# The gradient of the gate's taps: from full 128-channel blocks to 32-channel blocks at four column positions

## The chip, the cores and the metric

The kernel runs on one core of one Trainium2 chip. The metric is the device time of one launch in microseconds. The core has a matrix engine (PE, with its weight loads shown apart as PEld), a vector engine (DVE), a scalar engine (ACT), GpSimd (POOL), and a queue engine (SP) that issues most of the DMAs.

## The reference

The reference is the forward pass of a branchformer block and its gradients. B = 2 sequences of T = 4000 tokens have D = 144 channels, and the convolutions have K = 5 taps:

```
xa  = layernorm(x)
q, k, v = xa @ w_qkv                      # full attention over 4000 tokens
glob = softmax(q k^T / sqrt(D)) v @ w_att_out
u, g = gelu(xa @ w_mlp_in)                # two halves of 144 channels
g   = layernorm(g)
gc  = sum_i shift(g, i) * dw_csgu[i]      # 5 taps per channel: the gate
loc = (u * gc) @ w_mlp_out
m   = concat(glob, loc);  m = m + depthwise_conv(m, dw_merge)
out = x + m @ w_merge
```

It returns the output and the gradients of x and of all weights. The one that matters here is the gradient of `dw_csgu`, 5 x 144 numbers: for tap i and channel c it is the sum over all tokens t of g[t + i - 2, c] times the gradient of gc[t, c].

## The kernel before

A sequence is 32 blocks of 125 tokens, block j holding tokens p*32 + j for p = 0 to 124. The attention phase (`phase_att`) goes through 64 row tiles of 125 tokens, one per step s, 32 for each sequence. In a step the kernel computes the scores of tile s and the gradient of the probabilities of tile s - 1 (`quad`, L1186 and L1193: eight matmuls, of which four use all 128 rows and four use 16 rows each at four row positions), the softmax (L1208 on DVE, L1214 on ACT), the product with the gradient (L1224 on ACT, L1225 on DVE), two transposes by DMA (`PT`, `ST`), the products with them (`yz`, L1235 and L1274), and the accumulation of the gradient of the normalised input (`X_group`, L1330, added by DVE at L1337).

Beside attention runs the local branch (`local_units`): for sequence 0 in steps 2 to 26, for sequence 1 in steps 34 to 60. It works on groups of two blocks, and it is a list of small units that the steps take in equal shares. `ring` holds, for each block, the normalised gate g (`ring[:, 0]`) and the gradient of gc (`ring[:, 1]`), so that a block's five shifted copies are five neighbouring slots.

After every second group the tap gradient is taken for four blocks. The kernel multiplies `ring[:, 1]` of a block, as weights, with the five shifted blocks of `ring[:, 0]`, all 128 x 128 channel pairs, of which only the diagonal is wanted in the end. `dwc_unit(g, 0)` does four matmuls of 128 x 512 (four taps; L707). `dwc_unit(g, 1)` does, for each of the four blocks, one of 128 columns (the fifth tap; L709) and one for the last 16 channels, with channels 32 to 143 as weights and 80 columns (L710). Each sums in a PSUM buffer of the pool `ps_w`, which has three buffers and is shared with X, the projections and the gate. `flush` then copies the PSUM tile to `fl` on ACT (L693) and adds it on POOL to `A.dwc` (L694), a 128 x 720 accumulator in SBUF. `dwi_unit` does the same for the gradient of `w_mlp_in` (L722), with the same `fl`. A unit of the tap gradient runs 8 times per sequence, 16 times in all.

At the very end `Final.dwc` takes the diagonals: five DVE operations of 128 x 128 with the identity (L1831), five of 16 x 16 (L1833), two casts, two transposes on PE, one copy, one DMA.

The order of the instructions on each engine is written out: `Planner.ORDER` has one list per engine. The program is first emitted in program order and cut into runs. A run is one instruction, or on PE up to 16 consecutive matmuls into one tensor, or up to eight score matmuls. `plan` then chains the runs in the order of the list.

Of the kernel before, what the change touches and what calls it, by code (L numbers as in the profile page):

```python
# [8 lines left out]
BF = mybir.dt.bfloat16  # L9
F32 = mybir.dt.float32  # L10
ACT = mybir.ActivationFunctionType
ALU = mybir.AluOpType
# [3 lines left out]
D = 144  # L16
DR = 16
# [498 lines left out]
G2 = 2  # L516
# [5 lines left out]
def local_units(k, W, b, S, A, es, DHT, ps_w, gw):  # L522

    nc, tc = k.nc, k.tc
# [5 lines left out]
    ring = pl.tile([PB, 2, 16, D], BF, name="ring")  # L530
# [25 lines left out]
    fl = pl.tile([128, 512], F32, name="l_fl")  # L556
# [134 lines left out]
    def flush(ps, r0, r1, acc):  # L691
        n = ps.shape[1]
        nc.scalar.copy(fl[r0:r1, 0:n], ps)  # L693
        nc.gpsimd.tensor_tensor(acc, fl[r0:r1, 0:n], acc, op=ALU.add)  # L694

    def blocks(g):
        return [(g - 1, 0), (g - 1, 1), (g, 0), (g, 1)]

    def dwc_unit(g, part):
        pw = ps_w.tile([128, 512], F32, tag="w")  # L700
        bl = blocks(g)
        for n_, (gg, bi) in enumerate(bl):
            first, last = n_ == 0, n_ == len(bl) - 1
            t = ring[:, 1, (G2 * gg + bi + 2) % 12, :]
            p = (G2 * gg) % 12 + bi
            if part == 0:
                nc.tensor.matmul(pw[:].rearrange("p (a b) -> p a b", b=128), t[:, 0:128], ring[:, 0, p:p + 4, 0:128], start=first, stop=last)  # L707
            else:
                nc.tensor.matmul(pw[:, 0:128], t[:, 0:128], ring[:, 0, p + 4, 0:128], start=first, stop=last, skip_group_check=True)  # L709
                nc.tensor.matmul(pw[0:112, 128:208], t[:, 32:D], ring[:, 0, p:p + 5, 128:D], start=False, stop=last, skip_group_check=True)  # L710
        if part == 0:
            flush(pw[:], 0, 128, A.dwc[:, 0:512])
        else:
            flush(pw[:, 0:128], 0, 128, A.dwc[:, 512:640])
            flush(pw[96:112, 128:208], 96, 112, A.dwc[96:112, 640:720])

    def dwi_unit(g):
        pw = ps_w.tile([96, 3 * D], F32, tag="w")
        bl = blocks(g)
        for n_, (gg, bi) in enumerate(bl):  # L720
            for ct in range(3):
                nc.tensor.matmul(pw[:, ct * D:(ct + 1) * D], dhr[gg % 2][0:PB, bi, ct * 96:(ct + 1) * 96], S.xa_aug[:, G2 * gg + bi, 0:D],  # L722
                                 start=(n_ == 0 and ct == 0), stop=(n_ == len(bl) - 1), skip_group_check=True)
        flush(pw[:], 0, 96, A.dWiT[:])
# [6 lines left out]
    def round_(n, o):  # L731
# [4 lines left out]
        if o is not None and o % 2:  # L736
            end += [(dwc_unit, o, 0), (dwc_unit, o, 1), (dwi_unit, o)]
# [38 lines left out]
class Planner:  # L776

    ORDER = {
# [1156 lines left out]
def kernel(ctx, tc, x, w_qkv, w_att_out, w_mlp_in, dw_csgu, w_mlp_out, dw_merge, w_merge, grad_out,  # L1935
# [47 lines left out]
    A = K()  # L1983
# [194 lines left out]
```

## Time and profile before

| | before |
|---|---|
| median of 3 runs | 1206.63 us (1204.02 to 1208.19) |
| profiled execution | 1207.09 us, span of its instructions 1205.3 us |
| granted TensorE clock | 0.996 |
| PE, DVE, ACT, POOL busy | 1153.0, 1025.6, 934.5, 256.4 us |

Lines such as L707 are lines of the kernel. A row of a group gives line, engine, operation, output and input with shapes, the count, then the busy time in us and the mean of one in ns, then the idle time of that engine just before the group and what ended it. A row of the chain of waits gives the start in us, the length in us and what ran; pieces of the chain lie one behind another, so their lengths are times on the path that ended last. The ends of matmuls are modelled in the profile, so for PE the distance between starts, which the chain shows, says more than the duration of one.

### The profile page before, as it was taken

Reading aid. Unit: us, or ns where it says so; the run is one execution under the profiler, and the core shown is the slowest. Engines: PE = TensorE matmul, PEld = TensorE weight load, DVE = VectorE, ACT = ScalarE, POOL = GpSimd, SP = SyncE. Lnnn points to the kernel's source line nnn. Section 1 sums busy time; section 2 is a strip of 40 time slices with the busy share of each in tenths; the row PEclk is TensorE's granted clock in tenths of the full one; section 3 lists DMA queues with packets and bytes.
Section 4 is the critical chain, followed back from the end, with each engine's and each line's share of the span. In section 5 each row is a group of like instructions: output and inputs, shape, how many; then the busy total and the mean of one; then the engine's idle time right before and its main releaser. Section 6 shows DMA issues by size and latency. Waiting matters only on the chain.

```text
span 1205.3 us, 36108 instructions
## 1 busy us (share of the span) xinstructions
PE 1153.0 (96%) x14352; PEld 896.1 (74%) x14352; DVE 1025.6 (85%) x3035; ACT 934.5 (78%) x1705; POOL 256.4 (21%) x409
## 2 busy tenths in 40 slices
PE   6999999999999989999999999999999899999998
PEld 4667777777777767777777777777777677799997
DVE  8589899999999978778889999999999987667745
ACT  6999888898898765778998789788888657535372
POOL 7111112211212223200111121211112111023450
PEclk9999999999999999999999999999999999999999
DMA  4769888878778898878989888897888979868653
GB/s 116 167 151 181 168 166 170 155 177 163 170 169 160 156 193 175 165 155 187 211 166 171 156 161 168 159 165 156 172 160 150 173 155 179 191 153 212 147 143 89
DMA packets 672570, 198.31 MB, mean 165 GB/s; under 512 B 648339, under 2 KB 666313, under 8 KB 672379
## 3 DMA queue, kind: packets, MB, share of 16 engines
q1 hardware_dynamic: 671270, 194.60, 80.0%
q8 instruction: 112, 1.84, 0.7%
q0 software_dynamic: 592, 1.18, 0.5%
q14 instruction: 58, 0.48, 0.1%
q10 hardware_dynamic: 538, 0.21, 0.1%
HBM read 24.32 MB, written 17.85 MB: 35 GB/s over the span
## 4 chain that ended last, share of the span: by engine, by line
PE 63%; DMA 12%; ACT 11%; DVE 8%; issue 3%; SPq 2%; POOL 1%; DVEq 0%; ACTq 0%; POOLq 0%
PE X L1330 17%; PE ps L1186 12%; PE yz L1274 7%; DMA PT<-Pbuf 7%; PE yz L1235 7%; PE ps L1193 5%; ACT Pbuf L1214 3%; PE Hps L1617 3%; DVE Pbuf L1208 2%; ACT Sbuf L1224 2%; PE po L1715 2%; DMA qt<-qb 1%; DVE Sbuf L1225 1%; PE pd L606 1%; PE pj L1152 1%
## 5 line engine op out<-in xcount | busy, mean ns | idle before, releaser
L1208 DVE TENSOR_SCALAR_CACHE_REDUCE Pbuf<-ps 125x1000 bf16<-125x1000 f32 x256 | 306.5, 1198 | 49.9 <-PE ps L1193 45.1
L1224 ACT CAST Sbuf<-ps 125x1000 bf16<-125x1000 f32 x252 | 253.3, 1005 | 85.4 <-PE ps L1193 67.5
L1214 ACT ACTIVATE Pbuf<-Pbuf,nm 125x1000 bf16<-125x1000 bf16 x256 | 286.6, 1152 | 5.7 <-DVE nm L1210 5.5
L1330 PE MATMUL X<-QBs,Sbuf 125*128 125x144 bf16 x2048 | 280.6, 227 | 0.8 <-ACT l_sq L575 0.3
L1330 PE MATMUL X<-QBs,Pbuf 125*128 125x144 bf16 x2048 | 280.1, 226 | 0.7 <-POOL QBs L1257 0.7
L1186 PE MATMUL ps<-xaT_m,qt 128*128 128x500 bf16 x1024 | 262.4, 376 | 10.8 <-DVE Pbuf L1208 6.2
L1330 PEld LDWEIGHTS <-Sbuf 125*128 125x128 bf16 x2048 | 199.3, 98 | 16.0 <-issue 15.7
L1330 PEld LDWEIGHTS <-Pbuf 125*128 125x128 bf16 x2048 | 200.8, 98 | 2.3 <-issue 1.5
L1225 DVE TENSOR_TENSOR Sbuf<-Sbuf,Pbuf 125x1024 bf16<-125x1024 bf16 x252 | 172.7, 692 | 5.4 <-ACT Sbuf L1224 3.9
L1235 PE MATMUL yz<-xa_aug,PT 125*128 125x145 bf16 x2048 | 151.4, 228 | 16.4 <-DMA PT<-Pbuf 15.5
L1235 PEld LDWEIGHTS <-PT 125*128 125x128 bf16 x2048 | 130.9, 98 | 34.5 <-DMA PT<-Pbuf 22.4
L1274 PE MATMUL yz<-xa_aug,ST 125*128 125x144 bf16 x2048 | 151.1, 228 | 3.8 <-DMA ST<-Sbuf 2.7
L1186 PEld LDWEIGHTS <-qt 128*128 128x128 bf16 x1024 | 92.2, 98 | 77.0 <-issue 12.7
L1274 PEld LDWEIGHTS <-ST 125*128 125x128 bf16 x2048 | 133.0, 98 | 15.6 <-issue 9.0
L1257 POOL TENSOR_TENSOR QBs<-g,g 125x144 bf16<-125x144 f32 x64 | 37.8, 590 | 461.8 <-ACT g L1256 312.4
L1337 DVE TENSOR_TENSOR acc<-X,acc 125x432 f32<-125x432 f32 (+1 forms) x204 | 110.5, 548 | 22.3 <-PE X L1330 22.0
L1193 PEld LDWEIGHTS <-qt 16*128 16x128 bf16 x1024 | 26.3, 91 | 109.7 <-issue 109.7
L1193 PE MATMUL ps<-XR,qt 16*128 16x500 bf16 x1016 | 100.9, 381 | 0.0
L677 POOL TENSOR_SCALAR l_w<-ring,nc,c 125x144 f32<-125x144 bf16 x64 | 34.1, 539 | 165.8 <-DVE nc L673 93.6
L649 DVE TENSOR_TENSOR l_prod<-ring,Wc 125x720 bf16<-125x720 bf16 x128 | 66.1, 538 | 1.9 <-DMA ring<-held 1.6
L1742 ACT ACTIVATE t<-t,dx_c,rstd_x 125x144 f32<-125x144 f32 x64 | 29.2, 501 | 36.5 <-DVE t L1741 29.1
L1617 PE MATMUL Hps<-Yg,go_h 125*128 125x144 bf16 x640 | 54.3, 226 | 0.0
(540 smaller groups left out, 2031.8 us busy)
## 6 DMA issues: line engine op xcount, KB each, us to landing
Yn_d<-yn SPq DMA_DIRECT2D x64, 35.2 KB
Zn_d<-zn SPq DMA_DIRECT2D x64, 35.2 KB
ug_d<-ugr SPq DMA_DIRECT2D x32, 70.3 KB
PT<-Pbuf SPq DMA_TRANSPOSE x126
ST<-Sbuf SPq DMA_TRANSPOSE x126
acc_d<-acc SPq DMA_DIRECT2D x4, 504.0 KB
go_h<-in_grad_out_dram SPq DMA_DIRECT2D x8, 252.0 KB
Yg<-Yn_d SPq DMA_DIRECT2D x8, 252.0 KB
```

Of the source, the lines that this page charges most:

```text
L649: nc.vector.tensor_tensor(prod[:, bi].rearrange("p a b -> p (a b)"), ring[:, a, p + bi:p + bi + 5, :].rearrange("p a b -> p (a b)"), W.Wc[ ...
L1186: mm = nc.tensor.matmul(pp[r // 2][:, r % 2, 0:CH], QT[i][:, 2 * h, :], bs(i)[0].xaT_m[:, c * CH:(c + 1) * CH], start=True, stop=False)
L1193: nc.tensor.matmul(pp[r // 2][:, r % 2, 0:CH], QT[i][rs, 2 * h + 1, :], xr, start=False, stop=True)
L1208: nc.vector.tensor_scalar(pv(pc(i, c2)), src, -1.0, 3.0e38, op0=ALU.mult, op1=ALU.min, accum_out=NM[i][:, c2:c2 + 1])
L1214: nc.scalar.activation(v, v, ACT.Exp, bias=NM[i][:, 4:5], scale=-1.0)
L1224: nc.scalar.copy(pv(sc(i, c2)), src)
L1225: nc.vector.tensor_tensor(sc(i, c2), sc(i, c2), pc(i, c2), op=ALU.mult)
L1235: nc.tensor.matmul(Yw, PT[0:PB, pos(i, j), :], S.xa_aug[:, j, 0:D + 1], start=(j == 0), stop=(j == NB - 1))
L1274: nc.tensor.matmul(Zw, ST[0:PB, j, :], S.xa_aug[:, j, 0:D], start=(j == 0), stop=(j == NB - 1))
L1330: nc.tensor.matmul(X[:, jj, :], l, r, start=(n_ == 0), stop=(n_ == len(ops) - 1))
L1337: nc.vector.tensor_tensor(av, X[0:PB, 0:nj, :], av, op=ALU.add)
L1617: nc.tensor.matmul(H[0:rows, a // 3, (a % 3) * D:(a % 3 + 1) * D], lhs, self.src[b][h][:, 2 + j, :], start=(n == 0 and a % 3 == 0), stop=( ...
```

## The change

The 128 channels are cut into four blocks of 32. The weights of a matmul are 32 channels of `ring[:, 1]`, and its columns are the same 32 channels of the five shifted blocks of `ring[:, 0]`, 160 columns. The result of block c goes to PSUM partitions 32c to 32c + 31, and with that the matmul uses 32 of the array's columns, at one of four positions. Four blocks of tokens times four positions are 16 matmuls. The last 16 channels are done by four more matmuls, one for each block of tokens, each at a position of its own (channels 112 to 143 as weights, 80 columns), so that the four partial sums stay apart. The accumulator is 128 x 240, with one flush per unit. `Final.dwc` takes the diagonals of 32 x 32 blocks, and adds the four partial sums of the last 16 channels with two small matmuls, in two bfloat16 parts.

```diff
-    def dwc_unit(g, part):
-        pw = ps_w.tile([128, 512], F32, tag="w")
-        ...
-            if part == 0:
-                nc.tensor.matmul(pw[:].rearrange("p (a b) -> p a b", b=128), t[:, 0:128], ring[:, 0, p:p + 4, 0:128], start=first, stop=last)
-            else:
-                nc.tensor.matmul(pw[:, 0:128], t[:, 0:128], ring[:, 0, p + 4, 0:128], start=first, stop=last, skip_group_check=True)
-                nc.tensor.matmul(pw[0:112, 128:208], t[:, 32:D], ring[:, 0, p:p + 5, 128:D], start=False, stop=last, skip_group_check=True)
-        if part == 0:
-            flush(pw[:], 0, 128, A.dwc[:, 0:512])
-        else:
-            flush(pw[:, 0:128], 0, 128, A.dwc[:, 512:640])
-            flush(pw[96:112, 128:208], 96, 112, A.dwc[96:112, 640:720])
+    def dwc_unit(g):
+        pw = ps_w.tile([128, 240], F32, tag="w")
+        for q, (gg, bi) in enumerate(blocks(g)):
+            t = ring[:, 1, (G2 * gg + bi + 2) % 12, :]
+            p = (G2 * gg) % 12 + bi
+            for c in range(4):
+                nc.tensor.matmul(pw[32 * c:32 * c + 32, 0:160], t[:, 32 * c:32 * c + 32], ring[:, 0, p:p + 5, 32 * c:32 * c + 32], start=(q == 0), stop=(q == 3), skip_group_check=True)
+        for q, (gg, bi) in enumerate(blocks(g)):
+            ...
+            nc.tensor.matmul(pw[32 * q:32 * q + 32, 160:240], t[:, 112:D], ring[:, 0, p:p + 5, 128:D], start=False, stop=True, skip_group_check=True)
+        flush(pw[:], A.dwc[:])
...
-            end += [(dwc_unit, o, 0), (dwc_unit, o, 1), (dwi_unit, o)]
+            end += [(dwc_unit, o), (dwi_unit, o)]
...
+        for c in range(4):
+            nc.gpsimd.tensor_copy(dg[32 * c:32 * c + 32, :], W.ident[32 * c:32 * c + 32, 32 * c:32 * c + 32])
         for kk in range(5):
-            nc.vector.scalar_tensor_tensor(jf[:, 0:128], av[:, kk * 128:(kk + 1) * 128], 1.0, W.ident[:], ...)
-            nc.vector.scalar_tensor_tensor(jf[96:112, 0:DR], av[96:112, a0:a0 + DR], 1.0, W.ident[96:112, 96:112], ...)
+            nc.vector.scalar_tensor_tensor(jf[:, 0:32], av[:, kk * 32:(kk + 1) * 32], 1.0, dg[:], ...)
+            nc.vector.scalar_tensor_tensor(jf[:, 0:DR], av[:, a0:a0 + DR], 1.0, dg[:, DR:2 * DR], ...)
...
+        nc.tensor.matmul(pr[:], hi[:], dg[:, DR:2 * DR], start=True, stop=False)
+        nc.tensor.matmul(pr[:], lo[:], dg[:, DR:2 * DR], start=False, stop=True)
```

The five lists of `Planner.ORDER` are new throughout. Their lengths go from 1402, 2493, 1711, 405 and 937 runs (PE, DVE, ACT, POOL, SP) to 1402, 2495, 1680, 377 and 937. The local branch has one unit fewer for every second group, so the steps take its units at slightly other places of the program order.

More of the change, by code (lines that the diff above doesn't have):

```diff
@@ L555, in local_units @@
     w_ = pl.tile([PB, G2, D], F32, name="l_w")
-    fl = pl.tile([128, 512], F32, name="l_fl")
+    fl = pl.tile([128, 3 * D], F32, name="l_fl")
     def slot(g):
@@ L689, in dhT_unit, with flush @@
             DHT[G2 * g + bi] = [dhT[:, 3 * bi + ct, :] for ct in range(3)]
[L691 to L694, printed above, removed]
+    def flush(ps, acc):
+        r, n = ps.shape
+        nc.scalar.copy(fl[0:r, 0:n], ps)
+        nc.gpsimd.tensor_tensor(acc, fl[0:r, 0:n], acc, op=ALU.add)
     def blocks(g):
         return [(g - 1, 0), (g - 1, 1), (g, 0), (g, 1)]
-    def dwc_unit(g, part):
-        pw = ps_w.tile([128, 512], F32, tag="w")
-        bl = blocks(g)
-        for n_, (gg, bi) in enumerate(bl):
-            first, last = n_ == 0, n_ == len(bl) - 1
+    def dwc_unit(g):
+        pw = ps_w.tile([128, 240], F32, tag="w")
+        for q, (gg, bi) in enumerate(blocks(g)):
             t = ring[:, 1, (G2 * gg + bi + 2) % 12, :]
             p = (G2 * gg) % 12 + bi
-            if part == 0:
-                nc.tensor.matmul(pw[:].rearrange("p (a b) -> p a b", b=128), t[:, 0:128], ring[:, 0, p:p + 4, 0:128], start=first, stop=last)
-            else:
-                nc.tensor.matmul(pw[:, 0:128], t[:, 0:128], ring[:, 0, p + 4, 0:128], start=first, stop=last, skip_group_check=True)
-                nc.tensor.matmul(pw[0:112, 128:208], t[:, 32:D], ring[:, 0, p:p + 5, 128:D], start=False, stop=last, skip_group_check=True)
-        if part == 0:
-            flush(pw[:], 0, 128, A.dwc[:, 0:512])
-        else:
-            flush(pw[:, 0:128], 0, 128, A.dwc[:, 512:640])
-            flush(pw[96:112, 128:208], 96, 112, A.dwc[96:112, 640:720])
+            for c in range(4):
[5 more added lines that the diff above has]
+        flush(pw[:], A.dwc[:])
     def dwi_unit(g):
@@ L723, in dwi_unit @@
                                  start=(n_ == 0 and ct == 0), stop=(n_ == len(bl) - 1), skip_group_check=True)
-        flush(pw[:], 0, 96, A.dWiT[:])
+        flush(pw[:], A.dWiT[:])
     units = []
@@ L778 @@
     ORDER = {
[54 rows of a table removed]
-        "DVE": [2, 0, 3, 1, 4, 6, 7, 9, 8, 5, 11, 10, 12, 14, 15, 18, 16, 13, 17, 19, 22, 20, 25, 23, 24, 38, 44, 21, 32, 39, 36, 26, 28, 34, 33, 35,
[101 rows of a table removed]
-        "Activation": [1, 4, 0, 9, 10, 7, 8, 15, 34, 12, 11, 14, 13, 16, 39, 5, 42, 18, 19, 20, 3, 22, 21, 2, 23, 29, 28, 6, 24, 25, 17, 32, 26, 31,
[67 rows of a table removed]
-        "Pool": [4, 3, 2, 0, 5, 10, 8, 11, 6, 14, 7, 1, 15, 47, 16, 19, 18, 50, 41, 17, 26, 25, 24, 31, 32, 20, 33, 37, 38, 12, 34, 9, 27, 21, 13,
[48 rows of a table removed]
[54 rows of a table added]
+        "DVE": [2, 3, 0, 1, 4, 11, 5, 9, 10, 8, 7, 6, 12, 14, 15, 21, 16, 13, 17, 20, 22, 42, 24, 18, 44, 19, 25, 23, 32, 60, 34, 26, 28, 36, 33, 35,
[101 rows of a table added]
+        "Activation": [2, 4, 0, 1, 9, 10, 7, 8, 14, 13, 11, 5, 12, 18, 15, 16, 19, 17, 34, 20, 22, 21, 3, 41, 36, 23, 35, 6, 28, 24, 25, 26, 40, 29,
[65 rows of a table added]
+        "Pool": [5, 4, 47, 0, 1, 8, 6, 15, 14, 11, 49, 2, 10, 9, 16, 7, 18, 19, 17, 3, 26, 25, 24, 41, 33, 31, 32, 38, 13, 37, 42, 20, 28, 21, 23,
[47 rows of a table added]
     }
@@ L1828, in dwc @@
         self.jf = jf = fp.tile([128, D], F32, name="jf")
-        av = A.dwc
+        av, dg = A.dwc, fp.tile([128, 32], BF, name="dwc_d")
+        for c in range(4):
+            nc.gpsimd.tensor_copy(dg[32 * c:32 * c + 32, :], W.ident[32 * c:32 * c + 32, 32 * c:32 * c + 32])
         for kk in range(5):
-            nc.vector.scalar_tensor_tensor(jf[:, 0:128], av[:, kk * 128:(kk + 1) * 128], 1.0, W.ident[:], op0=ALU.mult, op1=ALU.mult, accum_out=dwc_c[:, kk:kk + 1])
-            a0 = 640 + kk * DR
-            nc.vector.scalar_tensor_tensor(jf[96:112, 0:DR], av[96:112, a0:a0 + DR], 1.0, W.ident[96:112, 96:112], op0=ALU.mult, op1=ALU.mult, accum_out=dwc_s[96:112, kk:kk + 1])
+            nc.vector.scalar_tensor_tensor(jf[:, 0:32], av[:, kk * 32:(kk + 1) * 32], 1.0, dg[:], op0=ALU.mult, op1=ALU.mult, accum_out=dwc_c[:, kk:kk + 1])
+            a0 = 160 + kk * DR
+            nc.vector.scalar_tensor_tensor(jf[:, 0:DR], av[:, a0:a0 + DR], 1.0, dg[:, DR:2 * DR], op0=ALU.mult, op1=ALU.mult, accum_out=dwc_s[:, kk:kk + 1])
         dwc_b = fp.tile([128, 5], BF, name="dwc_b")
         nc.vector.tensor_copy(dwc_b[:], dwc_c[:])
-        dwc_sb = fp.tile([128, 5], BF, name="dwc_sb")
-        nc.vector.tensor_copy(dwc_sb[96:112], dwc_s[96:112])
-        pt = self.pt([5, D], BF)
-        nc.tensor.transpose(pt[:, 0:128], dwc_b[:], W.ident[:])
-        nc.tensor.transpose(pt[:, 128:D], dwc_sb[96:112], W.ident[96:112, 96:112])
+        hi, lo, lof = fp.tile([128, 5], BF, name="dwc_hi"), fp.tile([128, 5], BF, name="dwc_lo"), fp.tile([128, 5], F32, name="dwc_lf")
+        nc.vector.tensor_copy(hi[:], dwc_s[:])
+        nc.vector.tensor_tensor(lof[:], dwc_s[:], hi[:], op=ALU.subtract)
+        nc.vector.tensor_copy(lo[:], lof[:])
+        pt = self.pt([5, 128], BF)
+        nc.tensor.transpose(pt[:], dwc_b[:], W.ident[:])
+        pr = self.pt([5, DR], F32)
+        nc.tensor.matmul(pr[:], hi[:], dg[:, DR:2 * DR], start=True, stop=False)
+        nc.tensor.matmul(pr[:], lo[:], dg[:, DR:2 * DR], start=False, stop=True)
         o5 = fp.tile([5, D], BF, name="o5")
-        nc.scalar.copy(o5[:], pt[:])
+        nc.scalar.copy(o5[:, 0:128], pt[:])
+        nc.scalar.copy(o5[:, 128:D], pr[:])
         nc.sync.dma_start(k.out5[:, :], o5[:])
@@ L1985 @@
     A.dWiT = ap.tile([96, 3 * D], F32, name="A_dWiT")
-    A.dwc = ap.tile([128, 720], F32, name="A_dwc")
+    A.dwc = ap.tile([128, 240], F32, name="A_dwc")
     k.ps_w = pool(ctx, "ps_w", "left", bufs=3, space=PSUM)
```

535 rows, old and new, of the table ORDER are left out of this document.

## The prediction

> **What bounds the kernel now.** I read the page first, then its chain of waits, then the same two stretches as a table of busy time.
>
> ```profile
> span 1205.3 us, 36108 instructions
> PE 1153.0 (96%) x14352; PEld 896.1 (74%) x14352; DVE 1025.6 (85%) x3035; ACT 934.5 (78%) x1705; POOL 256.4 (21%) x409
> PE 63%; DMA 12%; ACT 11%; DVE 8%; issue 3%; SPq 2%; POOL 1%; DVEq 0%; ACTq 0%; POOLq 0%
> 150.00:400.00 250.00, 247.80 (x3033) 188.38 (x3031) 241.56 (x709) 221.11 (x397) 50.62 (x73) 1.00 0.81 167
> 700.00:900.00 200.00, 196.38 (x2395) 149.09 (x2395) 188.14 (x542) 172.74 (x314) 38.66 (x58) 1.00 0.83 162
> ```
>
> The third line is the share of the chain by engine: TensorE matmuls carry 63% of what ends last. The last two are the middles of the two stages in which the local gate runs beside attention (columns: PE, PEld, DVE, ACT, POOL busy us). There PE has 2.2 and 3.6 us without work. DVE has 8.4 and 11.9 us: it is the next limit, some 4.5% away (20.3 of 450 us). The step that changes, the tap gradient, lies in these stages. One unit of it in the chain (start, us, what):
>
> ```profile
> 229.35 0.86 PE pw L707 x4
> 230.21 0.85 PE ps L1186 x4
> 231.06 0.32 PE ps L1193 x4
> 231.38 1.12 PE yz L1235 x16
> 232.50 0.06 PE pw L709
> 232.56 0.04 PE pw L710
> ...
> 232.87 0.85 PE ps L1186 x4
> ```
>
> The chain runs through PE without a gap here, so PE time removed here is removed from the end, until another engine is late. L707 is the first half of the unit, four matmuls of 512 columns, 0.86 us; L709 and L710 are the second, eight matmuls from 232.50 to 232.87, 0.37 us. Together 1.23 us, and 16 units make 19.7 us. Not all lie on the chain: it passes through L707 in 10 of the 16 units and through L709/L710 in 11; first and last of each:
>
> ```profile
> 134.31 0.86 PE pw L707 x4
> 137.47 0.06 PE pw L709
> ...
> 992.88 0.86 PE pw L707 x4
> 994.12 0.06 PE pw L709
> ```
>
> So I count 0.65 of what PE saves as lying on the path.
>
> **The matmuls.** The unit streams the same columns as before: 4×(512+128+80) = 2880 before, 16×160 + 4×80 = 2880 after. It gains only if the four column positions work at once. No row of this trace has column positions. The nearest has row positions: in the same chain L1186 and L1193 are four matmuls of 500 columns each, 0.85 us one after another on the whole array, and 0.32 us for L1193, whose four use four separate groups of 16 rows. They do overlap. By columns, a full-array matmul costs 0.85/4/500 = 0.425 ns a column, so 160 columns cost 68 ns and 80 columns 34 ns. If four run at once a unit is 4×68 + 34 = 0.31 us, or 4.9 us for 16 units. If all run one after another it is 16×68 + 4×34 = 1.22 us, or 19.6 us: nothing gained. I take the first, because L1193 is the row with the same kind of instruction (part of the array, different positions, back to back). The Trainium skill (TensorE: Matmul & The Clock Gate, Measured speedup vs the span model) gives 2.38 times for three column positions; at that efficiency of 0.79 a unit would be 0.39 us, 6.2 us in all, an estimate that hardly moves the sum.
>
> **Entering and leaving the positions.** L1193 also shows what a change of positions costs. Here a matmul group follows it directly:
>
> ```profile
> 182.35 0.32 PE ps L1193 x4
> 182.68 0.97 PE pw L707 x4
> 183.65 1.01 PE yz L1274 x16
> 184.66 0.85 PE ps L1186 x4
> 185.51 0.32 PE ps L1193 x4
> 185.83 1.12 PE yz L1235 x16
> ```
>
> L707 takes 0.97 behind row positions and 0.86 elsewhere; sixteen yz matmuls take 1.12 and 1.01. So one change costs 0.11 us, and the one into row positions is in L1193's own 0.32 (500 columns alone are 0.21). The new PE list decides how many are added. Numbering its runs in the order in which the program emits them, I find that the 20 matmuls of a unit are two runs, of 16 and of 4. They are neighbours in 9 units and apart in 7; in 15 of 16 the run of 16 stands right behind a group of score matmuls that ends in row positions, and so do the separated runs of 4. There the change is paid already, so each visit adds one, and the odd unit one more: 9 + 2×7 + 1 = 24 changes, 2.6 us. The after-cost is 4.9 + 2.6 = 7.5 us, so PE saves 12.2 us; one after another it would lose 19.6 + 2.6 − 19.7 = 2.5 us. On the path at 0.65 that is 7.9 saved, or 1.6 lost.
>
> **The weight loads.** Twelve loads a unit become twenty of 32 channels.
>
> ```profile
> L1193 PEld LDWEIGHTS <-qt 16*128 16x128 bf16 x1024 | 26.3, 91 | 109.7 <-issue 109.7
> L710 PEld LDWEIGHTS <-ring 125*112 125x112 bf16 x64 | 6.6, 132 | 0.0
> L1235 PE MATMUL yz<-xa_aug,PT 125*128 125x145 bf16 x2048 | 151.4, 228 | 16.4 <-DMA PT<-Pbuf 15.5
> L1235 PEld LDWEIGHTS <-PT 125*128 125x128 bf16 x2048 | 130.9, 98 | 34.5 <-DMA PT<-Pbuf 22.4
> ```
>
> The L1235 loads take 98 ns, yet sixteen load-and-matmul pairs took 1.01 us, 63 ns a pair, and L710 is followed after 0.04 us in spite of a load of 132 ns. Loads run under the matmuls before them, so I charge nothing; if that cover is missing, each of a unit's five rounds waits some 0.09 us (L1193's load). That is a rival below.
>
> **The flush.** One copy and one addition a unit replace three of each.
>
> ```profile
> L693 ACT COPY l_fl<-pw 128x512 f32<-128x512 f32 x16 | 9.3, 581 | 7.2 <-PE pw L707 5.9 <-PE X L1330 1.2
> L693 ACT COPY l_fl<-pw 128x128 f32<-128x128 f32 x16 | 4.3, 266 | 3.5 <-PE pw L710 3.4 <-POOL A_dwc L694 0.2
> L693 ACT COPY l_fl<-pw 16x80 f32<-16x80 f32 x16 | 3.5, 218 | 3.1 <-POOL A_dwc L694 2.8
> L694 POOL TENSOR_TENSOR A_dwc<-l_fl,A_dwc 128x512 f32<-128x512 f32 x16 | 21.2, 1326 | 55.1 <-ACT l_fl L693 55.1
> L694 POOL TENSOR_TENSOR A_dwc<-l_fl,A_dwc 128x128 f32<-128x128 f32 x16 | 8.6, 538 | 20.2 <-ACT l_fl L693 20.2
> L694 POOL TENSOR_TENSOR A_dwc<-l_fl,A_dwc 16x80 f32<-16x80 f32 x16 | 6.2, 388 | 1.5 <-ACT l_fl L693 0.3
> ```
>
> ACT: 581+266+218 = 1065 ns becomes one copy of 240 columns, by the line through the first two rows 266 + 112×0.82 = 358 ns; 11.3 us less over 16 units. POOL: 2252 ns becomes 538 + 112×2.05 = 768 ns, 23.7 us less. POOL is 21% busy, ACT 78%, so most is off the path; eleven pieces of L693 and L694 stand on the chain, 3.1 us in all, from
>
> ```profile
> 368.56 0.36 POOL A_dwc L694
> ...
> 967.02 0.15 ACT l_fl L693
> ```
>
> and since some belong to the flush of the other gradient, which stays, I take 1.5 us as gone. In the 7 separated units a PSUM buffer of the three is held between the two runs; the work queued behind would be X and the projections. It costs little as long as X finds buffers, as it does now (PE idle 0.8 us before 2048 matmuls):
>
> ```profile
> L1330 PE MATMUL X<-QBs,Sbuf 125*128 125x144 bf16 x2048 | 280.6, 227 | 0.8 <-ACT l_sq L575 0.3
> ```
>
> **The end.** The diagonal is taken from 32 columns instead of 128.
>
> ```profile
> L1831 DVE SCALAR_TENSOR_TENSOR jf<-A_dwc,ident x5: 278/285/286, 1079.7 to 1118.5; 128x128 f32<-128x128 f32 x5
> L1833 DVE SCALAR_TENSOR_TENSOR jf<-A_dwc,ident x5: 171/172/468, 1080.1 to 1130.0; 16x16 f32<-16x16 f32 x5
> L1835 DVE CAST dwc_b<-dwc_c x1: 159/159/159, 1147.8 to 1147.8; 128x5 bf16<-128x5 f32 x1
> ```
>
> Five of 285 ns become some 190 (between the two rows), −0.5 us; one cast becomes three small operations, +0.3; four small POOL copies, two tiny matmuls and one ACT copy are spread over 50 us in which ACT and POOL are mostly idle. I take zero, bounds −0.5 and +1.
>
> **The new lists.** All five queues are reordered. I counted the PE columns streamed between a tile's last score group and its first yz run, the cover for its softmax and the transposing DMA: 12.7 us a tile in the old list, 12.5 in the new. For the second transpose it is 5.5 and 6.2. So neither list covers clearly more, and I put the lists at 0 ± 4 us (a tile whose cover fails costs up to one transposition, 5.6 us):
>
> ```profile
> 277.09 5.62 DMA PT<-Pbuf
> ```
>
> **Sum.** 7.9 + 1.5 = 9.4 us leave the path. Late next is DVE, 4.5% away on average but in the same chain of buffers, so part comes back as DVE waits; I keep two thirds, 6.3 us. The profiled execution took 1207.1 us (span 1205.3 and 1.8 around it), 0.5 over the median of 1206.6. From the median: 1200.3 us.
>
> **Rivals.**
> - *Loads uncovered* (chance 0.14). Each round of four waits for its loads: 5×0.09 more a unit, 7.2 us in all, so PE saves 5.0 instead of 12.2; (5.0×0.65 + 1.5)×2/3 = 3.2 us, 1203.4. For it: L1193's loads do not start before the matmuls ahead end (109.7 us of idle). Against: the 63 ns pairs of L1235. The Trainium skill (TensorE: Matmul & The Clock Gate, The mechanism) says that a load overlaps a running matmul only when its row group differs, and column positions share their rows. By that rule this rival is what happens; the trace's L1235 pairs, which share all rows too, do not agree.
> - *One after another* (0.12). The four positions queue, and the changes come on top. It is slower when a load-and-matmul pair takes over (19.7 − 2.6)/16/20 = 53 ns; streamed serially it takes 61, which gives 1206.6 + 1.6 = 1208.2. With loads uncovered as well, 61 + 91 = 152 ns, PE loses (152 − 53)×320 ns = 32 us, 0.65 of it on the path, and the time is 1227. For it: no row shows column positions. Against: L1193. The Trainium skill (TensorEngine Tiling (Array Packing), Restrictions) adds that column tiling switches fast weight load off; no run here shows that yet.
> - *DVE takes over* (0.14). PE gets shorter but scores wait for the DVE's reading of the banks, and nothing arrives: 1206.6, ±2. For it: DVE at 241.56 of 250 us. Against: the gapless PE chain.
> - *The lists are worse* (0.10). Transposes come late once in several tiles; two more waits of 5.6 us outweigh the gain: 1206.6 − 6.3 + 11.2 = 1211.
>
> **How the numbers follow.** The forecast has 0.50. About 0.3% (3.6 us) can be told from no change, so faster means under 1203.0, slower over 1210.2. Forecast with its ±4 from the lists: 0.44 faster, 0.05 same, 0.01 slower; loads uncovered, with the same spread: 0.07, 0.06, 0.01; one after another: 0.02, 0.05, 0.05; DVE: 0.02, 0.10, 0.02; lists: 0.01, 0.02, 0.07. Sum 0.56, 0.28, 0.16. The range reaches from 1191 (all 12.2 and the 1.5 arrive, and 2 us from the lists) to 1211 (the last rival), and leaves out the uncovered serial case.
>
> **What would show it.** Right: the sixteen matmuls of a run start within 0.35 us, a unit takes some 0.42 us with its change, 0.11 us stands behind each run, L693 has one form of 128x240 near 360 ns, PE in the two stages has fewer idle us than DVE lost. Wrong: starts 60 ns or more apart (one after another), four starts together and then 0.15 us or more (loads), PE waiting for DVE L1208 by 6 us more than before (DVE), or more than two further yz waits for PT (lists).

## The result and the profile after

The changed kernel takes 1291.49 us (median of 4 runs, 1288.53 to 1294.57) against 1206.81 us in the same comparison: the ratio is 1.0705, with a 95% interval of 1.067 to 1.074. It is 85 us slower, where 6 us faster was forecast. The profiled execution took 1294.57 us, span 1292.8 us.

The part of the change that the prediction worked on did what was forecast. Here is one unit in the chain of waits of the changed kernel (start us, length us, what):

```profile
251.13 0.85 PE ps L1178 x4
251.98 0.32 PE ps L1185 x4
252.30 0.39 PE pw L705 x16
252.69 0.04 PE pw L709 x4
252.72 1.12 PE yz L1227 x16
```

The lines are renumbered: L1178 and L1185 are the old L1186 and L1193, L1227 the old L1235, L1266 the old L1274. The sixteen matmuls take 0.39 us. Of this 0.11 is the change from row positions, as forecast, so four rounds take 0.28; the last four take 0.04, and the yz group behind pays 0.11 for the way back (1.12 instead of 1.01). The four column positions work at once.

The time went somewhere else. From the page of the changed kernel: the queue of the hardware DMAs (packets, MB, share of 16 engines), the chain by engine, and the groups that wait for the two large transposes (busy us, mean ns | idle before, releaser):

```profile
q1 hardware_dynamic: 671270, 194.60, 83.0%
PE 44%; DMA 28%; ACT 11%; DVE 9%; issue 3%; SPq 3%; POOL 2%; ACTq 0%; POOLq 0%; DVEq 0%
L1227 PE MATMUL yz<-xa_aug,PT 125*128 125x145 bf16 x2048 | 157.2, 233 | 54.5 <-DMA PT<-Pbuf 53.3
L1266 PE MATMUL yz<-xa_aug,ST 125*128 125x144 bf16 x2048 | 152.8, 230 | 27.5 <-DMA ST<-Sbuf 27.1
```

Before, PE waited 15.5 us for PT there and DMA held 12% of the chain. For ST the row before was:

```profile
L1274 PE MATMUL yz<-xa_aug,ST 125*128 125x144 bf16 x2048 | 151.1, 228 | 3.8 <-DMA ST<-Sbuf 2.7
q1 hardware_dynamic: 671270, 194.60, 80.0%
```

The same number of packets and bytes took 0.830×1292.8 = 1073 us of the 16 engines instead of 0.800×1205.3 = 964. So it is not only a question of when the transposes are issued: the same transfers take longer. The instruction in the SP queue says so too. These are the rows of the two transposes in the views of the tiles PT and ST (ns min/median/max, first and last start), of the kernel before and then of the changed one:

```profile
L1218 SPq DMA_TRANSPOSE PT<-Pbuf x126: 1479/1719/3640, 33.1 to 1034.4; - x126
L1413 SPq DMA_TRANSPOSE ST<-Sbuf x126: 1496/1738/4199, 50.1 to 1040.3; - x126
```

```profile
L1210 SPq DMA_TRANSPOSE PT<-Pbuf x126: 1685/2447/4494, 30.7 to 1113.8; - x126
L1405 SPq DMA_TRANSPOSE ST<-Sbuf x126: 1527/2277/4696, 52.5 to 1131.0; - x126
```

The medians went from 1719 to 2447 and from 1738 to 2277 ns. The diff touches no transpose. But it makes the accumulator `A.dwc` smaller, from 2880 to 960 bytes in each partition, and the tiles allocated behind it on the left side of SBUF all move down by 1920 bytes, which is 7.5 times 256. Before, `Pbuf`, `Sbuf`, `PT` and `ST` started on multiples of 256 bytes (Pbuf at address 50944 of its partition); after, they start 128 bytes off (Pbuf at 49024). A large transpose reads 2048 rows of 256 bytes from Pbuf or Sbuf.

Three theories were put against each other. By the **address theory** the off starts make each transpose slower. By the **order theory** the new lists bunch the transposes or need them earlier. By the **column theory** the column positions slow the engine or its neighbours.

### The profile page after: what moved, and what is told of

Read it like the earlier page. It is cut to its first block, busy times and chain, and to the rows that moved or that the text cites. A ratio compares the mean times of both kernels' runs of the same rounds, so it can differ in the third digit from the quotient of the medians.

```text
span 1292.8 us, 36294 instructions
## 1 busy us (share of the span) xinstructions
PE 1168.1 (90%) x14481; PEld 903.3 (70%) x14481; DVE 1025.5 (79%) x3037; ACT 926.6 (72%) x1674; POOL 230.1 (18%) x381
## 4 chain that ended last, share of the span: by engine, by line
PE 44%; DMA 28%; ACT 11%; DVE 9%; issue 3%; SPq 3%; POOL 2%; ACTq 0%; POOLq 0%; DVEq 0%
DMA PT<-Pbuf 14%; PE X L1322 11%; PE ps L1178 9%; DMA ST<-Sbuf 8%; PE yz L1227 7%; PE yz L1266 5%; ACT Pbuf L1206 4%; PE ps L1185 3%; DVE Pbuf L1200 2%; ACT Sbuf L1216 2%; DMA qt<-qb 2%; DMA go_h<-in_grad_out_dram 1%; PE po L1707 1%; DVE Sbuf L1217 1%; PE Hps L1609 1%
## 5 line engine op out<-in xcount | busy, mean ns | idle before, releaser
L1200 DVE TENSOR_SCALAR_CACHE_REDUCE Pbuf<-ps 125x1000 bf16<-125x1000 f32 x256 | 306.6, 1198 | 61.2 <-PE ps L1185 58.8
L1178 PE MATMUL ps<-xaT_m,qt 128*128 128x500 bf16 x1024 | 269.3, 385 | 16.8 <-DMA qt<-qb 11.1
L1227 PE MATMUL yz<-xa_aug,PT 125*128 125x145 bf16 x2048 | 157.2, 233 | 54.5 <-DMA PT<-Pbuf 53.3
L1227 PEld LDWEIGHTS <-PT 125*128 125x128 bf16 x2048 | 135.5, 100 | 74.6 <-DMA PT<-Pbuf 67.4
L1266 PE MATMUL yz<-xa_aug,ST 125*128 125x144 bf16 x2048 | 152.8, 230 | 27.5 <-DMA ST<-Sbuf 27.1
L1266 PEld LDWEIGHTS <-ST 125*128 125x128 bf16 x2048 | 133.3, 99 | 43.2 <-DMA ST<-Sbuf 34.6
L1178 PEld LDWEIGHTS <-qt 128*128 128x128 bf16 x1024 | 93.2, 100 | 82.8 <-issue 13.3
L1185 PEld LDWEIGHTS <-qt 16*128 16x128 bf16 x1024 | 26.4, 91 | 113.2 <-issue 113.2
L1185 PE MATMUL ps<-XR,qt 16*128 16x500 bf16 x1016 | 101.7, 385 | 0.0
L1233 DVE RECIPROCAL rl<-yz 125x1 f32<-125x1 f32 x64 | 10.7, 167 | 60.9 <-PE yz L1227 60.7
```

The source lines that it names most:

```text
L1178: mm = nc.tensor.matmul(pp[r // 2][:, r % 2, 0:CH], QT[i][:, 2 * h, :], bs(i)[0].xaT_m[:, c * CH:(c + 1) * CH], start=True, stop=False)
L1185: nc.tensor.matmul(pp[r // 2][:, r % 2, 0:CH], QT[i][rs, 2 * h + 1, :], xr, start=False, stop=True)
L1200: nc.vector.tensor_scalar(pv(pc(i, c2)), src, -1.0, 3.0e38, op0=ALU.mult, op1=ALU.min, accum_out=NM[i][:, c2:c2 + 1])
L1227: nc.tensor.matmul(Yw, PT[0:PB, pos(i, j), :], S.xa_aug[:, j, 0:D + 1], start=(j == 0), stop=(j == NB - 1))
L1266: nc.tensor.matmul(Zw, ST[0:PB, j, :], S.xa_aug[:, j, 0:D], start=(j == 0), stop=(j == NB - 1))
```

## The experiments

**The old addresses with the new kernel.**

```diff
-    A.dwc = ap.tile([128, 240], F32, name="A_dwc")
+    A.dwc = ap.tile([128, 720], F32, name="A_dwc")[:, 0:240]
```

> The changed kernel with the accumulator tile allocated at its old 720 columns, of which 240 are used, so that every tile behind it on that side of SBUF is back at its old address. Address theory (the 1920 bytes saved moved the tiles of the transposing DMAs off multiples of 256 bytes and made each transpose slower): 1196 to 1205 us, the SP queue's PT<-Pbuf transpose back from a median of 2447 to about 1720 ns, PE yz waits for PT back from 53 to under 25 us. Order theory (the new lists issue or need the transposes at worse times): 1280 to 1295 us. Column theory (matmuls at column positions slow the engine around them): 1280 to 1295 us.

Measured: 1195.35 us (6 runs), ratio to the kernel before 0.9932 (0.9919 to 0.9946); the time lies a little under the range of the address theory. The loss is gone, with all lists and all column positions in place. The text below calls this kernel the aligned kernel. (The buffer `fl` of the flush is smaller by 320 bytes too, which moves tiles on the other side of SBUF. That stays so here and costs nothing that shows.) The transposes and the waits of its trace:

```profile
L1210 SPq DMA_TRANSPOSE PT<-Pbuf x126: 1468/1836/3878, 30.1 to 1016.2; - x126
L1405 SPq DMA_TRANSPOSE ST<-Sbuf x126: 1481/1772/4341, 50.1 to 1032.2; - x126
```

```profile
PE yz L1227 <- DMA PT<-Pbuf: 7.5, 12, 1.4
PE yz L1266 <- DMA ST<-Sbuf: 5.1, 7, 1.3
```

The second pair is from the list of waits (us in total, times, longest). PE waits 7.5 us for PT, less than the 15.5 of before. The median of the PT row is back at 1836 ns, not quite at the 1719 of before.

**The old kernel with shifted addresses.** The 128 bytes of `mhalf` go to the other side of SBUF.

```diff
-    k.mhalf = k.wpool.tile([128, 32], F32, name="mhalf")
-    k.goT = pool(ctx, "gt", "right").tile([128, (NB + 4) * 128], BF, name="goT")
+    gt = pool(ctx, "gt", "right")
+    k.mhalf = gt.tile([128, 32], F32, name="mhalf")
+    k.goT = gt.tile([128, (NB + 4) * 128], BF, name="goT")
```

> The kernel before, with one 128-byte tile (mhalf) moved from the left side of SBUF to the right, so that everything behind it on the left, the tiles of the transposes among it, starts 128 bytes lower; lists and computation are those of before. Address theory: 1270 to 1300 us and PT<-Pbuf near 2450 ns in the queue. Order and column theory: 1204 to 1210 us, PT<-Pbuf near 1720 ns.

Measured: 1286.7 us (4 runs), ratio 1.0687 (1.0671 to 1.0702). Nothing of the change is in this kernel, and it loses what the changed kernel loses. From its page and the views of its tiles:

```profile
PE 49%; DMA 28%; ACT 8%; DVE 8%; SPq 3%; issue 3%; POOL 1%; ACTq 0%; DVEq 0%; POOLq 0%
L1235 PE MATMUL yz<-xa_aug,PT 125*128 125x145 bf16 x2048 | 154.2, 230 | 49.7 <-DMA PT<-Pbuf 46.5
...
L1218 SPq DMA_TRANSPOSE PT<-Pbuf x126: 1521/2398/3973, 33.1 to 1113.3; - x126
L1413 SPq DMA_TRANSPOSE ST<-Sbuf x126: 1591/2181/4286, 51.6 to 1120.2; - x126
```

DMA again holds 28% of the chain and PE waits 46.5 us for PT. These two runs settle it: order and column theory are out for the 85 us.

The granted clock went down as well, and it too could cost time. It was 0.978 in the profiled execution of the changed kernel, 0.990 in this one and 0.996 before. The share that was not granted, times the span, bounds what that can have cost: an estimate of 28 us, 13 us and 5 us. So at most 13 of the 83 us here can have come by way of the clock, and at most 28 of the 85 in the changed kernel. In all runs of this case it was under 0.992 only where both sources were off.

**How many bytes off.** In the first of these runs the accumulator has 272 columns (128 bytes more than in the change), in the second 256 (64 more).

```diff
-    A.dwc = ap.tile([128, 240], F32, name="A_dwc")
+    A.dwc = ap.tile([128, 272], F32, name="A_dwc")[:, 0:240]
```

> The changed kernel with 128 bytes added behind the accumulator (272 columns): Pbuf, Sbuf, PT and ST start on multiples of 512 bytes, where before they started on odd multiples of 256. If the grain is 256 bytes, the same time as with 720 columns within 4 us. If what matters is the old address itself, or its place within 512 bytes, over 1250 us. Order theory: 1280 to 1295 us.

> The changed kernel with 64 bytes behind the accumulator (256 columns): Pbuf, Sbuf, PT and ST start 192 bytes past a multiple of 256, which is a multiple of 64. If every start off 256 bytes costs the same (a row of 256 bytes then touches two 256-byte lines): 1270 to 1295 us. If a multiple of 64 is enough: 1190 to 1200. If the price follows the distance to the line: 1225 to 1265.

Measured, one run each: 1194.93 us with 272 columns (starts on multiples of 512) and 1290.77 us with 256 (192 bytes past a multiple of 256). So the old address itself does not matter. A multiple of 256 is enough, as the run with 720 columns shows, a multiple of 64 is not, and 192 bytes off cost what 128 do.

The Trainium skill (DMA: Bandwidth & Descriptors, How a descriptor splits into AXI transactions) says that a transaction has to start on a 256-byte boundary, so that a transfer that starts off one fetches bytes which it does not use. The runs agree on the boundary. By that page's beats of 32 bytes a 256-byte row would cost 12 instead of 8 when it starts 128 bytes off and 14 when it starts 192 bytes off, an estimate; the two runs show no such difference (1291.49 and 1290.77 us). Nor does every row get longer: of the 256-byte packets of the large PT transposes 2% took more than 18 ns in the kernel before and 20% in the changed one, and the rest stayed at or below that.

**Which side, source or destination.** A gap of 128 bytes is put ahead of `PT`; once with the change as it is (only the sources Pbuf and Sbuf stay off), once with 272 columns and a second gap behind `ST` (only PT and ST are off).

```diff
+    gap0 = ab.tile([128, 64], BF, name="gap0")
     PT = ab.tile([128, NB, 128], BF, name="PT")
     ST = ab.tile([128, NB, 128], BF, name="ST")
```

> The changed kernel as it is (Pbuf and Sbuf, the sources of the two large transposes, stay 128 bytes off a multiple of 256), with a gap of 128 bytes behind them, so that the destinations PT and ST and everything behind lie as in the run with 272 columns, PT and ST on multiples of 256. If the read side costs: 1280 to 1295 us. If the write side costs: 1190 to 1200. If both do: 1225 to 1265.

> The changed kernel with 272 columns (Pbuf and Sbuf on multiples of 512) and a gap of 128 bytes ahead of PT and another behind ST, so that only PT and ST are 128 bytes off. If the read side costs: 1190 to 1200 us. If the write side costs: 1280 to 1295. If both do: 1225 to 1265.

Measured, one run each: 1290.66 us with the sources off, 1196.14 us with the destinations off. The cost is on the read side. Where the transpose writes shows no cost: 1196.14 lies among the runs of the aligned kernel (1194.33 to 1197.86). The SP queue's rows, sources off and then destinations off:

```profile
L1211 SPq DMA_TRANSPOSE PT<-Pbuf x126: 1636/2399/4523, 30.8 to 1111.5; - x126
```

```profile
L1212 SPq DMA_TRANSPOSE PT<-Pbuf x126: 1467/1858/4013, 30.3 to 1018.8; - x126
```

**One source at a time.** A gap between `Pbuf` and `Sbuf` leaves only Pbuf off; with 272 columns, one there and one behind Sbuf, only Sbuf.

```diff
     Pbuf = ab.tile([128, NPS, 1024], BF, name="Pbuf")
+    gap0 = ab.tile([128, 64], BF, name="gap0")
     Sbuf = ab.tile([128, NDS, 1024], BF, name="Sbuf")
```

> The changed kernel as it is, with a gap of 128 bytes between Pbuf and Sbuf, so that only Pbuf, the source of PT, starts 128 bytes off a multiple of 256; Sbuf, PT and ST start on multiples. If each transpose from an off start costs the same and the costs add up: half of the 95 us, 1235 to 1250 us. If one slow transpose a tile is enough to hold up the step: 1270 to 1290. If the path has room for one slow transpose a tile: 1195 to 1215.

> The changed kernel with 272 columns, a gap of 128 bytes between Pbuf and Sbuf and another behind Sbuf, so that only Sbuf, the source of ST, starts 128 bytes off. Costs that add up: 1235 to 1250 us, and with the run in which only Pbuf is off the two losses sum to some 95 us. One is enough: 1270 to 1290. Room for one: 1195 to 1215.

Measured, one run each: 1235.03 us with Pbuf off and 1231.89 with Sbuf off, 39.7 and 36.5 us over the 1195.35 of the kernel with aligned starts. (The kernel before took 1205.81 us beside these two and 1204.05 beside the aligned one, so each may be some 2 us less.) The second is under the range for costs that add up. The two single losses sum to 76 us, where both sources at once cost 95 (1290.66): at once they cost a quarter more. The granted clock may have a part in that (0.984 with both off, 0.993 and 0.994 with one); by the estimate above it can have cost at most 21 us there, against 9 and 7. The cause stays open. In the run with Pbuf off the tiles ahead of it (`acc` and `rstd_x`) are off too; in the one with Sbuf off nothing else of the large transposes is. The views of PT and ST with only Pbuf off:

```profile
L1211 SPq DMA_TRANSPOSE PT<-Pbuf x126: 1507/2266/4491, 30.2 to 1054.2; - x126
L1406 SPq DMA_TRANSPOSE ST<-Sbuf x126: 1472/1750/4126, 51.7 to 1071.2; - x126
```

Only the transpose whose source is off is slow in the queue: 2266 ns for PT, 1750 for ST. With Sbuf off it is less clean (PT 2017, ST 2082 ns). The packets of the traces tell it more directly. From the first transpose on, only transposes have packets of 256 bytes in this queue, 2048 for each PT and ST, and in order of time they divide exactly among the transposes. Here is the time from a transpose's issue to the end of its last packet (us):

| kernel | PT shortest, median | ST shortest, median |
|---|---|---|
| before | 3.07, 3.37 | 3.07, 3.37 |
| changed | 3.71, 3.97 | 3.70, 4.00 |
| aligned (720 columns) | 3.07, 3.35 | 3.07, 3.38 |
| 192 bytes off (256 columns) | 3.71, 4.01 | 3.70, 3.95 |
| only destinations off | 3.07, 3.38 | 3.07, 3.41 |
| only Pbuf off | 3.71, 3.90 | 3.07, 3.38 |
| only Sbuf off | 3.07, 3.56 | 3.69, 3.87 |

The shortest ones, which were held up least, are some 0.63 us longer whenever their own source is off, and never otherwise. With only Sbuf off the median of PT goes up, but its shortest does not, so the PT transposes are held up there and not slowed themselves. There are 252 large transposes, so at the end of the kernel one from an off source costs 95.3/252 = 0.38 us, some 0.6 of what it is longer.

**The matmuls alone.** To see what the column positions are worth, the aligned kernel was run with full-array matmuls in their place, in the same places of the same lists. This kernel leaves out the wanted gradient of the taps.

```diff
-                nc.tensor.matmul(pw[32 * c:32 * c + 32, 0:160], t[:, 32 * c:32 * c + 32], ring[...], start=(q == 0), stop=(q == 3), ...)
+                nc.tensor.matmul(pw[:, 0:160], t[:, 0:128], ring[...], start=(q == 0 and c == 0), stop=(q == 3 and c == 3), ...)
...
-            nc.tensor.matmul(pw[32 * q:32 * q + 32, 160:240], t[:, 112:D], ring[...], start=False, stop=True, ...)
+            nc.tensor.matmul(pw[:, 160:240], t[:, 0:128], ring[...], start=False, stop=True, ...)
```

> The changed kernel with 720 columns allocated, but the 20 matmuls of a unit use the first 128 channels as weights on the full array, so they run one after another and no position changes are added (this leaves the wanted gradient out: its columns hold other products). Lists and flush are those of the change. PE needs 16 x (16 x 68 + 4 x 34) = 19.6 us for them instead of 7.5. If the PE saving reaches the end as forecast (0.43 of it): 5 us over the padded kernel. If DVE takes it all: within 1.5 us. If all of it counts: 12 us over.

Measured: 1205.51 us (12 runs), 1.0011 of the kernel before (0.9995 to 1.0028), 10.2 us over the aligned kernel. A unit in the two timelines of PE, one after another and then at column positions (start, length, what):

```profile
138.61 1.28 PE L705 MATMUL pw<-ring 125*128 125x160 bf16 x16
139.73 0.31 PE L709 MATMUL pw<-ring 125*128 125x80 bf16 x4
139.87 1.18 PE L1227 MATMUL yz<-xa_aug,PT 125*128 125x145 bf16 x16
```

```profile
139.25 0.46 PE L705 MATMUL pw<-ring 125*32 125x160 bf16 x16
139.54 0.21 PE L709 MATMUL pw<-ring 125*32 125x80 bf16 x4
139.68 1.19 PE L1227 MATMUL yz<-xa_aug,PT 125*128 125x145 bf16 x16
```

From the first matmul to the group behind, the unit takes 1.26 us on the full array and 0.43 us at column positions. All of the measured gain of the aligned kernel is in these matmuls: lists, flush and final part together come out at a ratio of 1.0011, an interval that includes no change. Those three were not run apart.

**All transposes aligned.** Three gaps more put the tiles of the small transposes (qb, qt, zn, zt, dhr, dhT) on multiples of 256. They were 64 to 160 bytes off in the kernel before, and off in the aligned kernel.

```diff
+    gap1 = ab.tile([128, 96], BF, name="gap1")
     qbr = [ab.tile([128, 512], BF, name="qb%d" % i) for i in range(3)]
...
+    gap2 = ab.tile([128, 80], BF, name="gap2")
...
-    fl = pl.tile([128, 3 * D], F32, name="l_fl")
+    fl = pl.tile([128, (3 * D, 488)[b == 0]], F32, name="l_fl")
```

> The changed kernel with 272 columns and three further gaps (192 and 160 bytes on the left, 224 in fl on the right), so that the tiles of the small transposes (qb to qt, zn to zt, dhr to dhT) start on multiples of 256 too; they were 64 to 160 bytes off in the kernel before and in all runs so far. They move 72 of 588 thousand rows of 256 bytes. If their starts cost as much per row as the large ones (some 92 us for 516 thousand rows) and lie on the path as much: 1181 to 1188 us. If their time is hidden: 1193 to 1197.

Measured: 1197.48 us (12 runs), ratio 0.9957 (0.9933 to 0.998). That is no better than the aligned kernel without them (0.9932), and half a microsecond over the range for a hidden time. The small transposes did get shorter: from issue to last packet the shortest qt went from 1.95 to 1.80 us and the shortest dhT from 2.27 to 2.03. So their time is hidden. The version that beats both is the change with its sources on multiples of 256, at 0.9932.

## Why the prediction was wrong

**The step that failed** is the list of what the change touches. The part-by-part working costed matmuls, loads, flush, end and lists, and left out the allocation. The accumulator's 1920 bytes were in the diff, and everything behind it moved. The 5.62 us of a PT transpose was used as a constant of the kernel (under the new lists and in the last rival), when the time of a transpose depends on where its source starts: 3.07 us from issue to last packet at the shortest before, 3.71 after. So a term of some 95 us stood at nothing (1290.66 with the sources off against 1195.35). With the starts put back the kernel is at 0.9932, that is 1198.4 us from the median of 1206.6, beside the forecast of 1200.3. That it comes so near is in part luck: the forecast had 5.3 us from the matmuls and 1.0 from the flush, and the runs show 10.2 and nothing that can be seen.

**Matmuls and changes: right.** Forecast were 0.31 us for the matmuls of a unit and 0.42 with the change; measured 0.28 + 0.04, and 0.43 with the change. The change costs 0.11 us as the row positions had shown, in the way back to the yz group too. The rivals of uncovered loads and of one after another are out: four starts together, rounds 0.07 us apart.

**Flush: right in size, worth nothing that can be seen.** The copy was put at 358 ns and the addition at 768, a tenth too long. The changed kernel has

```profile
L694 POOL TENSOR_TENSOR A_dwc<-l_fl,A_dwc 128x240 f32<-128x240 f32 x16 | 11.1, 693 | 85.9 <-ACT l_fl L693 82.6 <-PE pw L717 3.2
L693 ACT COPY l_fl<-pw 128x240 f32<-128x240 f32 x16 | 5.7, 358 | 22.3 <-PE pw L709 22.2
```

The 1.5 us taken as gone from the chain do not show in the run without column positions, though new lists that lose as much could hide them.

**The share that arrives: too small.** Of PE's 12.2 us the forecast let 0.65 lie on the path and kept two thirds of that, 0.43. In the traces of the run without column positions and of the aligned one, the 16 units take 20.2 and 7.7 us of PE from their first matmul to the group behind, 12.5 apart (by the forecast's counts 19.6 − 7.5 = 12.1). The time differs by 10.2: 0.81 arrives. DVE had the room. In the same two stages the aligned kernel has

```profile
150.00:400.00 250.00, 248.66 (x3137) 190.51 (x3135) 245.39 (x728) 221.80 (x394) 43.56 (x64) 1.00 0.84 169
700.00:900.00 200.00, 197.71 (x2486) 150.66 (x2485) 191.81 (x557) 173.91 (x307) 30.89 (x48) 1.00 0.84 164
```

DVE's time without work fell from 20.3 to 4.6 + 8.2 = 12.8 us: it did become busier, and was not the bound. In the aligned kernel's list of waits PE waits 7.2 us for DVE's L1200; before it was 6.2 for the same line, so the rival in which DVE takes over is out too. The share of the units that lie on one chain was a poor measure of the path. A likely reason, which no run shows, is that where PE has no gaps, a unit that the chain happens to pass by delays what the chain waits for later.

**The lists: right at 0 ± 4, as far as they can be told from the flush.** Old matmul time with the new lists and the new flush gives 1.0011.

**The signs to watch** held one that pointed at the loss: more than two further yz waits for PT. There were 20 before and 47 after. But the prediction would have read them as the lists' doing; the length of the transpose, in the SP queue and from issue to last packet, tells the two apart.

## What to carry to other kernels

A change in the size of a tile moves every tile that is allocated behind it: compare the start addresses before and after, and keep the sources of large DMA transposes on multiples of 256 bytes, by a pad if need be. When a wait for a transfer grows, look first at whether the transfer was issued later or took longer, since the queue's own rows and its packets answer that. Where an engine runs without gaps, do not count its saved time by how many of its instructions one chain happens to show: here 0.81 of it arrived, where that count, cut by a third for DVE, had said 0.43.

## What was not expected of the hardware

- A large DMA transpose whose source starts 128 or 192 bytes off a multiple of 256 takes some 0.63 us more from issue to last packet at the shortest (3.07 to 3.70 us), and costs 0.38 us at the end of this kernel, 95 us over 252 of them. Where its destination starts makes no difference that shows (1196.14 against 1195.35 us, 3.07 us each).
- Four column positions with all 125 rows run at the full rate at once, each with its own columns read: 160 columns at four positions take 0.07 us a round, as long as one such matmul on the full array.
- The granted clock was 0.978 in the profiled execution of the changed kernel and 0.997 in the aligned one. It was lowest where PE waited longest; whether the waits are the reason was not tried.
